# Second chunk's attention as a pinned pair-by-pair pipeline, keys' maxima by GpSimd, second weight converted by halves

## The chip, the cores and the metric

One core of a Trainium2 chip runs the kernel. The metric is the device time of one execution in microseconds. Engines of the core: TensorE (PE in the rows, its weight loads PEld), VectorE (DVE), ScalarE (ACT), GpSimd (POOL), and SyncE (SP), which here only issues DMAs. Each engine takes its own queue of instructions strictly in order; engines wait for each other by semaphores.

## The reference, cut to what matters

```python
q_s = softmax(q, over the head dimension)            # 8 batches, 8 heads, 576 tokens, 64 wide
k_s = softmax(k, over the 576 tokens)
kv = einsum('bhsd,bhse->bhde', k_s, v)
x = einsum('bhsd,bhde->bhse', q_s, kv)               # as 4608 tokens x 512
h = x @ w_in;  x = maximum(0.01 * h, h) @ w_out      # 512 -> 2048 -> 512, weights in float64
h = maximum(maximum(x @ w1, x @ w2), x @ w3); out = h @ w_out2   # 512 -> 768 -> 512
```

## The kernel before

The 4608 tokens stand in nine chunks of 512 (`NC`), a chunk reaching over one or two batches (`_pieces`). Heads go by pairs, so four pairs (`hp`) fill the 128 partitions. Attention of a batch and pair is a generator `kv_unit` (keys: maximum over the tokens, exponential, product with the values, division), that of a chunk and pair is `q_unit` (maximum, exponential, sum, division, four transposes on TensorE, product with the keys' result, split into a high and a low part, `xhi` and `xlo`). Products in float32 quality are three products of such parts (`mm3`): high by high, high by low, low by high.

The first wide product (w_in, w_out) is cut into 16 blocks (`MA`). Each block's weights come as 64-bit words in a tile `raw` and are converted by `split_words` to a high and a low part in a tile `w`, of which half `s = 0` belongs to w_in and half `s = 1` to w_out (`parts`). The conversion is one ScalarE pass (L172, absolute value), seven VectorE passes over 1024 columns (L173 to L185, with L184 the whole value and L185 the low part) and a ScalarE pass for the high part (L177); a ScalarE copy of half the whole values (L188) and a DMA from ScalarE's queue (L189) then keep w_in's whole values in HBM. All conversions use the one buffer `ca`.

A step is one block of one chunk: `project` (12 products of 512 columns into a bank `ps`), ScalarE's Prelu `g`, its parts `ghi` and `glo`, and `a_out` (12 products into four banks `acc`). `TURNS` sets the steps' order: chunk 0 with block 0 (step 0), then chunk 1 with blocks 0 and 1 (steps 1 and 2), chunk 0 with blocks 1 to 3 (steps 3 to 5), and so on; `BEGUN` says at which step the conversion of a block is begun. Chunk 0's attention runs first, alone. The attention of chunk 1 (batch 1, units in `second`) starts while step 0 runs; its units advance side by side, stage by stage (`advance`). After them the second block's conversion (`conv_a(1, ...)`) is written, then the third's.

In batch 0 and batch 1 the keys' maxima come from TensorE transposes (L415) and VectorE reductions (L420 to L422); for batch 1 they go back to all partitions as a diagonal times ones (L426, L429) and are added on VectorE (L431). From batch 2 on, VectorE takes the maximum of the five key tiles (L444, L446), GpSimd reduces it over the partitions (`partition_all_reduce`, L447), and VectorE subtracts (L452). The queues' order comes from a scheduler that works on the written order and its own forecast; instructions that are handed to `pin` (`keep_in_program_order`) keep their written order.

## Time and profile before

| What | us |
|---|---|
| median of 3 runs (1401.33 to 1402.17) | 1401.95 |
| profiled execution, whole time | 1401.96 |
| its span in the trace | 1400.1 |
| TensorE busy in the span | 1379.7 (99%) |
| VectorE busy | 865.4 (62%) |
| ScalarE busy | 673.3 (48%) |
| GpSimd busy | 156.4 (11%) |

The whole time is 1.86 us more than the span, and equals the median of the runs to 0.01 us. Times below are from the span's start. A duration in a row of the timeline is that of all instructions in the row from the first one's start to the last one's end; consecutive instructions of one engine overlap by some 0.08 us where the second doesn't need the first.

### The profile page before, as it was taken

What the parts mean: (1) busy time and instruction counts of PE and PEld (TensorE: products, weight loads), DVE (VectorE), ACT (ScalarE), POOL (GpSimd) and SP (SyncE); (2) the same over time, 40 slices, a digit from 0 to 9 for tenths busy, and PEclk for the clock granted to TensorE, in tenths of its full rate; (3) what the DMA queues carried; (4) which work ended last, traced back from release to release, by engine and by line L of the source; (5) the groups of instructions that cost most, each with busy time, mean ns of one, the idle gap of its engine ahead of it and who ended that gap; (6) DMA issues with size and microseconds to landing.
All of it is one profiled execution on the core that took longest, in us unless ns stands there. A gap on an engine that the chain in (4) does not pass through costs nothing.

```text
span 1400.1 us, 18335 instructions
## 1 busy us (share of the span) xinstructions
PE 1379.7 (99%) x6624; PEld 1127.8 (81%) x6624; DVE 865.4 (62%) x1500; ACT 673.3 (48%) x1387; POOL 156.4 (11%) x261
## 2 busy tenths in 40 slices
PE   7999999999999999999999999999999999999998
PEld 5788877788888788888888888888888888888887
DVE  9888978864786885656657455676457255434311
ACT  7766867754676656645445344334224224322211
POOL 0000202200111130110223300110010000000000
PEclk9999999999999999999999999999999999999999
DMA  9388864635977866768788797665673573554601
GB/s 368 129 284 305 300 224 132 220 108 206 386 287 269 366 215 233 285 215 351 242 338 326 284 359 268 237 225 173 228 260 135 210 293 120 173 218 158 237 26 38
DMA packets 90826, 330.10 MB, mean 236 GB/s; under 512 B 10672, under 2 KB 27056, under 8 KB 67568
## 3 DMA queue, kind: packets, MB, share of 16 engines
q1 hardware_dynamic: 68512, 251.46, 48.8%
q0 software_dynamic: 19056, 66.98, 14.0%
q10 hardware_dynamic: 3168, 10.49, 1.9%
q8 instruction: 52, 0.85, 0.2%
q14 instruction: 38, 0.31, 0.1%
HBM read 253.66 MB, written 75.24 MB: 235 GB/s over the span
## 4 chain that ended last, share of the span: by engine, by line
PE 89%; DVE 5%; ACT 3%; issue 1%; DMA 1%; POOL 0%; ACTq 0%; SPq 0%; DVEq 0%; POOLq 0%
PE ps L867 40%; PE acc L639 34%; PE ps L639 13%; PE ps L461 1%; PE ps L591 1%; ACT qo L527 0%; DVE glo L660 0%; DMA stream<-room 0%; DVE qmx L534 0%; DVE qsm L549 0%; DVE nmx L420 0%; ACT ghi L659 0%; DVE spare L546 0%; DVE spare L557 0%; PE ps L571 0%
## 5 line engine op out<-in xcount | busy, mean ns | idle before, releaser
L867 PE MATMUL ps<-op,group 128*128 128x512 f32 x1512 | 352.2, 389 | 0.0
L867 PEld LDWEIGHTS ps<-op,group 128*128 128x128 f32 x1512 | 283.7, 188 | 59.1 <-ACT snap L1099 0.2
L639 PE MATMUL acc<-ghi,outw 128*128 128x512 f32 x768 | 248.0, 391 | 0.9 <-ACT ghi L659 0.6
L867 PE MATMUL ps<-opA,group 128*128 128x512 f32 x1008 | 247.4, 391 | 0.8 <-ACT opA L827 0.6
L867 PEld LDWEIGHTS ps<-opA,group 128*128 128x128 f32 x1008 | 187.9, 188 | 41.5 <-ACT snap L995 1.5
L639 PEld LDWEIGHTS acc<-ghi,outw 128*128 128x128 f32 x768 | 143.7, 188 | 32.2 <-ACT ghi L659 1.6
L639 PE MATMUL acc<-glo,outw 128*128 128x512 f32 x384 | 150.5, 392 | 0.6 <-DVE glo L660 0.2
L639 PE MATMUL acc<-wo,h 128*128 128x512 f32 x558 | 135.6, 389 | 0.0
L639 PE MATMUL ps<-xhi,w 128*128 128x512 f32 x384 | 125.8, 394 | 1.3 <-ACT g L917 0.7
L639 PE MATMUL acc<-ghi,w 128*128 128x512 f32 x384 | 127.0, 393 | 0.0
L1099 ACT ACTIVATE snap<-ps 128x512 f32<-128x512 f32 x108 | 61.9, 597 | 134.6 <-PE ps L867 134.4
L639 PEld LDWEIGHTS acc<-wo,h 128*128 128x128 f32 x558 | 104.7, 188 | 21.8
L660 DVE TENSOR_TENSOR glo<-g,ghi 128x512 fp32r<-128x512 f32 x102 | 69.7, 687 | 74.4 <-ACT ghi L659 74.0
L1114 DVE TENSOR_TENSOR snap<-snap,ps 128x512 f32<-128x512 f32 x72 | 49.2, 685 | 93.2 <-ACT snap L1099 69.9
L639 PEld LDWEIGHTS ps<-xhi,w 128*128 128x128 f32 x384 | 72.1, 188 | 17.5 <-ACT g L917 1.1
L639 PEld LDWEIGHTS acc<-glo,outw 128*128 128x128 f32 x384 | 72.1, 188 | 17.3 <-DVE glo L660 2.6
L659 ACT ACTIVATE ghi<-g 128x512 fp32r<-128x512 f32 x102 | 63.4, 630 | 45.9 <-DVE g L1299 27.3
L639 PEld LDWEIGHTS acc<-ghi,w 128*128 128x128 f32 x384 | 71.8, 188 | 15.3
L1110 DVE TENSOR_TENSOR best<-snap,ps 128x512 f32<-128x512 f32 x36 | 24.7, 687 | 87.7 <-PE ps L867 39.2
L639 PE MATMUL acc<-glo,w 128*128 128x512 f32 x192 | 75.5, 393 | 0.8 <-DVE glo L660 0.8
L639 PE MATMUL ps<-xlo,w 128*128 128x512 f32 x192 | 74.9, 391 | 0.1
L1123 ACT ACTIVATE h<-best 128x512 fp32r<-128x512 f32 x48 | 30.3, 630 | 87.6 <-DVE best L1116 87.2
(188 smaller groups left out, 1917.2 us busy)
## 6 DMA issues: line engine op xcount, KB each, us to landing
group<-stream SPq DMA_DIRECT2D x62, 1024.0 KB, 6.2
outw<-stream_out SPq DMA_DIRECT2D x48, 1024.0 KB, 8.5
group<-stream_in SPq DMA_DIRECT2D x42, 1024.0 KB, 7.7
stream<-room POOLq DMA_DIRECT2D x66, 256.0 KB, 5.8
raw<-in_wa_dram SPq DMA_DIRECT2D x16, 1024.0 KB, 7.7
x<-st SPq DMA_DIRECT2D x40, 256.0 KB, 3.4
room<-in_wb_dram POOLq DMA_DIRECT2D x18, 512.0 KB, 8.0
stream_out<-w SPq DMA_DIRECT2D x16, 512.0 KB, 4.3
```

The costliest lines, as they stand in the source:

```text
L461: nc.tensor.matmul(acc[z, : D + 1], lhsT=ke[:, r, z], rhs=vt[:, r, h], start=r == 0, stop=r == RK - 1)
L591: nc.tensor.matmul(both(xps, c0, c1), lhsT=a, rhs=halves(y, c0, c1), start=i == 0, stop=i == 2)
L639: nc.tensor.matmul(acc, lhsT=l, rhs=r, start=first and i == 0, stop=last and i == 2)
L659: nc.scalar.activation(hi[:, z], g[:, z], AF.Copy)
L660: nc.vector.tensor_tensor(lo[:, z], g[:, z], hi[:, z].bitcast(F32), op=ALU.subtract)
L867: nc.tensor.matmul(bank, lhsT=l, rhs=r, start=fresh and first, stop=last, skip_group_check=not fresh)
L1099: nc.scalar.activation(t, bank, AF.Copy)
L1110: nc.vector.tensor_tensor(g, snap, bank, op=ALU.add)
L1114: nc.vector.tensor_tensor(snap, snap, bank, op=ALU.add)
L1123: nc.scalar.activation(h[:, m, 0], g, AF.Copy)
```

## The change

Five things are edited. First, `split_words` writes the whole values into the raw words' own tile, and their store goes out from SyncE's queue; ScalarE's copy is gone. Second, keys of batch 1 take the way of the later batches: four maxima per pair on VectorE, a reduction by GpSimd, one subtraction; the transposes, the diagonal and its product are gone for that batch. A reduction of one column is issued on GpSimd at the start. Third, the queries of chunk 1 are objects `EarlyQuery`, whose stages `finish_second` writes out in a fixed, pinned order, pair after pair, each pair's last stages among the next pair's first ones. Their loads are issued behind the loads of batch 1's keys and values and behind the store of block 0's whole values. Fourth, block 1 is converted by `split_by_halves`: the same operations, over 512 columns each, w_in's half before w_out's, with the high part made by VectorE (a cast) in place of ScalarE. Its VectorE work is written behind the last pair. Fifth, the four stores of step 0 are pinned, and so is the first product of step 2.

```diff
     def split_words(raw, hi, lo, n, after=None, whole=None, keep=None):
...
-        nc.vector.tensor_tensor(af, af, bf, op=ALU.add)
-        nc.vector.tensor_tensor(lo, af, hi.bitcast(F32), op=ALU.subtract)
+        z = raw.bitcast(F32)[:, :n]
+        nc.vector.tensor_tensor(z, af, bf, op=ALU.add)
+        nc.vector.tensor_tensor(lo, z, hi.bitcast(F32), op=ALU.subtract)
         if keep is not None:
-            copy = raw.bitcast(F32)[:, :N]
-            nc.scalar.activation(copy, af[:, :N], AF.Copy)
-            pin(nc.scalar.dma_start(keep, copy))
+            nc.sync.dma_start(keep, z[:, :N])
+    def split_by_halves(raw, hi, lo, keep):
...
+        for i in range(2):
+            z = slice(i * N, i * N + N)
+            pin(nc.scalar.activation(a[:, z].bitcast(F32), words[:, z, 1].bitcast(F32), AF.Abs))
+            yield
+        for i in range(2):
+            z = slice(i * N, i * N + N)
...
+            pin(nc.vector.tensor_scalar(af, af, MOST_HIGH, LEAST_HIGH, op0=ALU.min, op1=ALU.max))
+            nc.vector.tensor_scalar(au, au, 3, 0x3FFFFFF8, op0=ALU.logical_shift_left, op1=ALU.bitwise_and)
+            nc.vector.scalar_tensor_tensor(au, high, 0xC0000000, au, op0=ALU.bitwise_and, op1=ALU.bitwise_or)
+            nc.vector.tensor_copy(hi[:, z], af)
+            nc.vector.tensor_scalar(high, au, 0xFF800000, None, op0=ALU.bitwise_and)
+            nc.vector.scalar_tensor_tensor(bf, low, 2.0**-52, bf, op0=ALU.mult, op1=ALU.mult)
+            whole = raw.bitcast(F32)[:, 2 * i * N : 2 * i * N + N]
+            nc.vector.tensor_tensor(whole, af, bf, op=ALU.add)
+            nc.vector.tensor_tensor(lo[:, z], whole, hi[:, z].bitcast(F32), op=ALU.subtract)
+            if i == 0:
+                nc.sync.dma_start(keep, whole)
+        yield
...
+    pin(nc.gpsimd.partition_all_reduce(ones, ones, P, bass_isa.ReduceOp.max))
...
-        if b < FIRST:
+        if b == 0:
...
-            if b == 1:
-                diag = ap.tile([P, P], F32, tag="mx", name="diag", bufs=2)
-                nc.scalar.activation(diag, ident, AF.Copy, scale=mx[:, 0:1])
-                yield
-                spread = psum()
-                nc.tensor.matmul(spread[:, :P], lhsT=ones, rhs=diag, start=True, stop=True)
-                yield
-                nc.vector.tensor_tensor(ke, ke, spread[:, None, :P].to_broadcast([P, RK, P]), op=ALU.add)
-                nc.scalar.activation(ke, ke, AF.Exp)
...
+    class EarlyQuery:
...
+            nc.sync.dma_start(self.qt, q[1, hp])
+        def shift(self):
+            pin(nc.vector.tensor_reduce(mx, self.groups, axis=AX.X, op=ALU.max))
+            pin(nc.vector.tensor_tensor(self.groups, self.groups, self.spread(mx), op=ALU.subtract))
+            nc.scalar.activation(self.qt, self.qt, AF.Exp)
+        def normalise(self):
+            pin(nc.vector.tensor_reduce(sm, self.groups, axis=AX.X, op=ALU.add))
+            pin(nc.vector.tensor_scalar(sm, sm, EPS, None, op0=ALU.add))
+            pin(nc.vector.reciprocal(sm, sm))
+            pin(nc.vector.tensor_tensor(self.groups, self.groups, self.spread(sm), op=ALU.mult))
+            self.tp = psum()
+            for r in range(4):
+                pin(nc.tensor.transpose(self.tp[:, z], self.qt[:, z], ident))
+        def back(self):
+            pin(nc.scalar.activation(self.qt, self.tp, AF.Copy))
+        def multiply(self):
...
+        def high(self):
+            pin(nc.scalar.activation(xhi, self.xps, AF.Copy))
+            pin(nc.tensor.matmul(p, lhsT=minus, rhs=hi, start=False, stop=True, skip_group_check=True))
+        def low(self):
+                nc.vector.tensor_tensor(lo, p, hi.bitcast(F32), op=ALU.subtract)
+            pin(nc.scalar.activation(both(xlo, at, H), both(self.xps, at, H), AF.Copy))
...
+    def finish_second(keys, queries, convert):
+        keys = advance(keys, 2)
+        for z in queries[:2]:
+            z.shift()
+        advance(keys)
+        a_out(*prev, hold=True)
+        z = queries
+        z[0].normalise()
+        z[0].back()
+        z[2].shift()
+        z[0].multiply()
+        z[1].normalise()
+        z[0].high()
+        z[1].back()
+        z[0].low()
...
+        next(convert)
+        z[2].multiply()
+        z[3].normalise()
+        z[2].high()
+        z[3].back()
+        z[2].low()
+        z[3].multiply()
+        z[3].high()
+        z[3].low()
+        for _ in convert:
+            pass
...
-            acc = project(wA[m][0], x_tiles(c))
+            acc = project(wA[m][0], x_tiles(c), pinned=step == 2)
...
             if step == 0:
-                second = advance(second, 2)
-                a_out(*prev, hold=True)
+                finish_second(second_keys, second_queries, conv_by_halves(1))
                 prev = None
-                advance(second)
                 for f in range(KDM):
-                    store(f, x2[turn][:, f], accs[c][f], busy=True)
-                conv_a(1, spare(1, NP - 1))
+                    st = gp.tile([P, N], F32, tag="st", name="st", bufs=4)
+                    pin(nc.scalar.activation(st, accs[c][f], AF.Copy))
+                    nc.sync.dma_start(x2[turn][:, f], st)
                 conv_a(2, x_tiles(1)[0][:, NP - 1].bitcast(F32))
```

Three places of the built order show where instructions stand. Numbers are buffers: `w_416` (before) and `w_417` (after) hold block 0; `raw_445` with `w_724` (before) and `w_647` (after) hold block 1; `xhi_694`, `xlo_695` and `xhi_618`, `xlo_619` are chunk 1's parts; `ps_754`, `ps_787`, `ps_838` are the banks of steps 1, 2 and 3 before, and `ps_720`, `ps_752`, `ps_802` after; `spare_429` to `spare_438` (before) or `spare_435` (after) are the rooms of batch 1's four pairs.

VectorE, from the last division of batch 1's keys to the low part of block 1, before:

```order
L466 TENSOR_SCALAR rc_686<-ps_651 128x1
L467 RECIPROCAL rc_686<-rc_686 128x1
L173 TENSOR_SCALAR ca_725<-ca_725 128x1024
L174 TENSOR_SCALAR ca_725<-ca_725 128x1024
L175 SCALAR_TENSOR_TENSOR ca_725<-raw_445,ca_725 128x1024
L178 TENSOR_SCALAR raw_445<-ca_725 128x1024
L179 SCALAR_TENSOR_TENSOR raw_445<-raw_445 128x1024
L184 TENSOR_TENSOR ca_725<-ca_725,raw_445 128x1024
L623 TENSOR_TENSOR xlo_695<-ps_667,xhi_694 128x2x32
L623 TENSOR_TENSOR xlo_695<-ps_675,xhi_694 128x2x32
L623 TENSOR_TENSOR xlo_695<-ps_683,xhi_694 128x2x32
L185 TENSOR_TENSOR w_724<-ca_725,w_724 128x1024
```

The same place after, from the second pair's low part on:

```order
L669 TENSOR_TENSOR xlo_619<-ps_629,xhi_618 128x2x32
L632 TENSOR_REDUCE qsm_653<-spare_435 128x8
L633 TENSOR_SCALAR qsm_653<-qsm_653 128x8
L634 RECIPROCAL qsm_653<-qsm_653 128x8
L635 TENSOR_TENSOR spare_435<-spare_435,qsm_653 128x512
L669 TENSOR_TENSOR xlo_619<-ps_650,xhi_618 128x2x32
L669 TENSOR_TENSOR xlo_619<-ps_668,xhi_618 128x2x32
L202 TENSOR_SCALAR ca_648<-ca_648 128x512
L203 TENSOR_SCALAR ca_648<-ca_648 128x512
L204 SCALAR_TENSOR_TENSOR ca_648<-raw_445,ca_648 128x512
L205 CAST w_647<-ca_648 128x512
L206 TENSOR_SCALAR raw_445<-ca_648 128x512
```

Block 1's conversion, which stood ahead of all four low parts of chunk 1, now stands behind the last of them.

TensorE at the start of step 1, before:

```order
L619 MATMUL ps_667<-xhi_694,kvhi5_118 128x2x224
L619 MATMUL ps_675<-xhi_694,kvhi5_118 128x2x224
L619 MATMUL ps_683<-xhi_694,kvhi5_118 128x2x224
L619 MATMUL ps_691<-xhi_694,kvhi5_118 128x2x224
L639 MATMUL ps_754<-xhi_694,w_416 128x512
L639 MATMUL ps_754<-xlo_695,w_416 128x512
L639 MATMUL ps_754<-xhi_694,w_416 128x512 x2
L639 MATMUL ps_754<-xlo_695,w_416 128x512
L639 MATMUL ps_754<-xhi_694,w_416 128x512 x2
L639 MATMUL ps_787<-xhi_694,w_724 128x512
```

TensorE at the start of step 1, after:

```order
L648 MATMUL ps_668<-spare_435,plain_146 128x2x224
L715 MATMUL ps_720<-xhi_618,w_417 128x512
L715 MATMUL ps_720<-xlo_619,w_417 128x512
L715 MATMUL ps_720<-xhi_618,w_417 128x512 x2
L715 MATMUL ps_720<-xlo_619,w_417 128x512
L715 MATMUL ps_720<-xhi_618,w_417 128x512 x2
L715 MATMUL ps_720<-xlo_619,w_417 128x512
L715 MATMUL ps_720<-xhi_618,w_417 128x512
L662 MATMUL ps_668<-xhi_618,kvhi5_118 128x2x224
L715 MATMUL ps_720<-xhi_618,w_417 128x512
L715 MATMUL ps_720<-xlo_619,w_417 128x512
L715 MATMUL ps_720<-xhi_618,w_417 128x512
```

Nine of step 1's twelve products now stand ahead of the last pair's subtraction product (L662; L619 before), which its low part reads.

SyncE's queue of loads, before:

```order
L400 DMA spare_438<-in_k_dram 128x640
L513 DMA spare_438<-in_q_dram 128x512
L403 DMA spare_429<-in_v_dram 128x650
L403 DMA spare_432<-in_v_dram 128x650
L403 DMA spare_435<-in_v_dram 128x650
L403 DMA spare_438<-in_v_dram 128x650
L199 DMA raw_445<-in_wa_dram 128x1024
L199 DMA raw_447<-in_wa_dram 128x1024
```

And after:

```order
L428 DMA spare_435<-in_v_dram 128x650
L188 DMA wi0_149<-raw_185 128x512
L619 DMA spare_429<-in_q_dram 128x512
L619 DMA spare_431<-in_q_dram 128x512
L619 DMA spare_433<-in_q_dram 128x512
L619 DMA spare_435<-in_q_dram 128x512
L223 DMA raw_445<-in_wa_dram 128x1024
L223 DMA raw_447<-in_wa_dram 128x1024
```

The store of block 0's whole values, which waits for VectorE, now stands ahead of chunk 1's queries and of the raw words of blocks 1 and on.

## Rows read from the trace of the kernel before

**Rows 1.** Windows view: busy us (instructions) of each engine, clock, DMA share, GB/s.

```profile
60.00:70.00 10.00, 10.00 (x46) 7.99 (x45) 8.96 (x11) 6.51 (x12) 0.00 (x0) 1.00 0.49 180
```

**Rows 2.** Chain that ended last, from 46 us: start, us, engine, tile, line.

```profile
46.93 0.70 DVE ca L173
...
51.71 1.23 DVE ca L184
...
53.12 8.92 PE ps L639 x38
62.04 3.77 PE acc L639 x16
65.82 2.04 PE ps L639 x9
```

**Rows 3.** Timeline of VectorE: start, us, line, operation, tiles, shapes.

```profile
21.17 1.22 DVE L179 SCALAR_TENSOR_TENSOR raw<-raw 128x1024 f32<-128x1024 uint32 x1
...
62.66 1.22 DVE L185 TENSOR_TENSOR w<-ca,w 128x1024 fp32r<-128x1024 f32 x1
```

**Rows 4.** VectorE's groups by shape, first 200 us: busy us, mean ns of one.

```profile
L185 DVE TENSOR_TENSOR w<-ca,w 128x1024 fp32r<-128x1024 f32 x16 | 19.5, 1221 | 0.3
L660 DVE TENSOR_TENSOR glo<-g,ghi 128x512 fp32r<-128x512 f32 x26 | 17.9, 687 | 6.2 <-ACT ghi L659 5.9
L174 DVE TENSOR_SCALAR ca<-ca 128x1024 uint32<-128x1024 uint32 x16 | 11.1, 691 | 0.4
L446 DVE TENSOR_TENSOR mx<-mx,ke 128x128 f32<-128x128 f32 x12 | 3.4, 285 | 0.1
L452 DVE TENSOR_TENSOR ke<-ke,mx 128x640 f32<-128x640 f32 x4 | 3.2, 799 | 0.0
L556 DVE RECIPROCAL qsm<-qsm 128x8 f32<-128x8 f32 x12 | 2.3, 195 | 0.0
L467 DVE RECIPROCAL rc<-rc 128x1 f32<-128x1 f32 x12 | 1.9, 158 | 0.2
```

**Rows 5.** Timeline of TensorE, attention of chunks 0 and 1.

```profile
23.29 1.10 PE L571 MATMUL ps<-qf,plain 128*128 128x512 f32 x2 [0.42 <-issue]
...
39.62 0.60 PE L563 MATMUL ps<-ident,spare 128*128 128x128 f32 x4
...
52.08 0.48 PE L619 MATMUL ps<-xhi,kvhi 128*128 128x448 f32 x1 [0.67 <-ACT xhi L613]
...
67.47 0.39 PE L639 MATMUL ps<-xlo,w 128*128 128x512 f32 x1
```

**Rows 6.** Timeline of ScalarE, the same stretch.

```profile
37.77 1.58 ACT L669 ACTIVATE st<-acc 128x512 f32<-128x512 f32 x3
...
48.23 0.60 ACT L565 ACTIVATE qf<-ps 128x512 f32<-128x512 f32 x1
...
51.45 0.58 ACT L613 ACTIVATE xhi<-ps 128x512 fp32r<-128x512 f32 x1
```

**Rows 7.** DMA issues, first 40 us: KB each, median us to landing.

```profile
raw<-in_wa_dram SPq DMA_DIRECT2D x4, 1024.0 KB, 9.3
...
spare<-in_q_dram SPq DMA_DIRECT2D x8, 256.0 KB, 5.8
```

**Rows 8.** Timeline of all engines around two of GpSimd's reductions.

```profile
441.00 0.94 DVE L446 TENSOR_TENSOR mx<-mx,ke 128x128 f32<-128x128 f32 x3
...
442.12 0.70 POOL L447 PARTITION_ALL_REDUCE mx<-mx  x1 [5.87 <-ACT qo L527]
...
442.99 0.81 DVE L452 TENSOR_TENSOR ke<-ke,mx 128x640 f32<-128x640 f32 x1
...
499.14 1.22 DVE L828 TENSOR_TENSOR opA<-side,opA 128x1024 fp32r<-128x1024 f32 x1
499.41 2.12 POOL L447 PARTITION_ALL_REDUCE mx<-mx  x1 [8.21 <-DVE mx L446]
```

**Rows 9.** View of line L447: count, duration min/median/max in ns, first and last start.

```profile
L447 POOL PARTITION_ALL_REDUCE mx<-mx x24: 657/699/2121, 134.8 to 544.1; - x24
```

More of the change, by code (lines that the diff above doesn't have):

```diff
@@ L121, in tile_kernel @@
         nc.vector.tensor_tensor(ident[z, z], column[z, 0], column[z, 1], op=ALU.is_equal)
-    ones = const.tile([P, P], F32, name="ones")
+    ones = const.tile([P, 1], F32, name="ones")
     nc.gpsimd.memset(ones, 1.0)
@@ L406, in kv_unit @@
             yield
-        if b < FIRST:
-            t4, t1 = (ps_acc.tile([P, N], F32, tag="acc", name="t") if i == b == 0 else psum() for i in range(2))
+        if b == 0:
+            t4, t1 = (ps_acc.tile([P, N], F32, tag="acc", name="t") if i == 0 else psum() for i in range(2))
             back = ke.rearrange("p r d -> p (r d)")
@@ L450, in kv_unit @@
                 behind_step(vt[:, 0, 0, 0:1])
-            fetch.dma_start(vt, v[b, hp])
+            if b >= FIRST:
+                fetch.dma_start(vt, v[b, hp])
             nc.vector.tensor_tensor(ke, ke, mx[:, None, :].to_broadcast([P, RK, P]), op=ALU.subtract)
@@ L632, in split_kv, with mm3, project @@
         nc.vector.tensor_tensor(lo, full, hi.bitcast(F32), op=ALU.subtract)
-    def mm3(acc, a, b, first, last):
+    def mm3(acc, a, b, first, last, pinned=False):
         prods = ((a[0], b[0]), (a[0], b[1]), (a[1], b[0]))
         for i, (l, r) in enumerate(prods):
-            nc.tensor.matmul(acc, lhsT=l, rhs=r, start=first and i == 0, stop=last and i == 2)
+            ins = nc.tensor.matmul(acc, lhsT=l, rhs=r, start=first and i == 0, stop=last and i == 2)
+            if pinned and i == 0:
+                pin(ins)
     def cols(pair, i, n=P):
         return tuple(t[:, i * n : (i + 1) * n] for t in pair)
-    def project(wslot, xpair):
+    def project(wslot, xpair, pinned=False):
         acc = psum()
         for kk in range(KDM):
-            mm3(acc, cols(wslot, kk), tuple(t[:, kk] for t in xpair), kk == 0, kk == KDM - 1)
+            mm3(acc, cols(wslot, kk), tuple(t[:, kk] for t in xpair), kk == 0, kk == KDM - 1, pinned and kk == 0)
         return acc
@@ L730, in conv_a, with conv_by_halves @@
         wA[m] = parts(tiles[m])
+    def conv_by_halves(m):
+        raw = words.pop(m)
+        if raw.dtype != I64:
+            yield
+            yield
+            tiles[m] = weights(raw, None, whole_in[m])
+            yield
+        else:
+            w = tiles[m] = wp.tile([P, 2, 2, N], F32R, tag="w", name="w")
+            yield from split_by_halves(raw, flat(w[:, 0]), flat(w[:, 1]), whole_in[m])
+        wA[m] = parts(tiles[m])
     def plan_units(c):
@@ L793, in first_units @@
         return [unit(c, hp, True) for hp in range(NP) for unit in (kv_unit, q_unit)]
+    def finish_second(keys, queries, convert):
[13 more added lines that the diff above has]
+        z[0].low()
+        z[3].shift()
+        z[1].multiply()
+        z[2].normalise()
+        z[1].high()
+        z[2].back()
+        z[1].low()
+        next(convert)
[9 more added lines that the diff above has]
+            pass
     def advance(units, stages=99):
@@ L803, in tile_kernel @@
     conv_a(0, None)
-    second = advance(first_units(1), 2)
+    second_keys = [kv_unit(1, hp, True) for hp in range(NP)]
+    advance(second_keys, 1)
+    advance(second_keys, 1)
+    second_queries = [EarlyQuery(hp) for hp in range(NP)]
     load_a(1)
```

49 lines of the change are left out of this document (40 added, 9 removed).

## Prediction, made blind

> **What bounds the kernel now.** I read the windows first: from 60 us TensorE is busy for all of each window, at a granted clock of 1.00 [rows 1], its upper level of 2.4 GHz. A microsecond that it loses there isn't won back, and one that it gains in the stretch before is a gain of the whole. So the change acts by one thing: when TensorE begins its closed row of products, and whether the row stays closed. In the chain, step 1's first product starts at 53.12; before it stand VectorE's passes for block 1, from 46.93 to 52.94 [rows 2], and in VectorE's queue chunk 1's low parts stand behind them. Thus before, block 1's conversion delays `xlo`, and TensorE pays for it. But then block 1 is ready as the row begins, and block 2's low part at 63.88 [rows 3], before TensorE asks for it: behind 53.12 come 38, 16 and 9 products without a pause [rows 2], so the 63rd starts at 67.47 [rows 5], one every 0.227 us.
>
> The reader is to see two needs of TensorE that VectorE serves in a row: chunk 1's parts, and blocks 1 and 2. The change puts the parts first.
>
> **The point at which both are compared.** By the built order, 62 products of steps 1 to 4 stand ahead of the first that reads block 2's low part in the changed kernel. In the kernel before, the 63rd starts at 67.47. I work out when it can start after.
>
> **VectorE up to the queries.** Up to the end of L179, at 22.4 [rows 3], the queue is the same. Then: two passes over 1024 columns for block 0 at 1.22, less the overlap 0.08, 2.3 us; 16 maxima of 0.285 [rows 4], 0.20 apart where pairs alternate and 0.32 where one needs the one before, 4.2; four subtractions of 0.80 [rows 4], 3.0 with overlap; eight small divisions, 0.6. VectorE waits for GpSimd once, 0.3 (a reduction's result is used 1.05 us after its last maximum, 441.94 to 442.99 [rows 8], and the next pair's maxima cover most), and for the first product of keys with values, behind an exponential and TensorE's queue, 0.9. Sum 11.3: the queries begin at 33.7.
>
> **The queries.** Per pair: maximum, subtraction, sum and multiplication at 0.69 [rows 4], an addition of 0.16 and a reciprocal of 0.20, with overlaps and hand-offs of 0.04, 3.1 us. Four pairs 12.4, the low part `glo` of step 0 0.6, four divisions 0.3, two low parts `xlo` 0.3. Twice VectorE stands before `xlo`: the pinned order puts the next pair's four transposes (0.60) ahead of the subtraction product (0.48) [rows 5], which `xlo` needs, 1.0 each time. Sum 15.6: the fourth pair's multiplication ends at 49.3.
>
> **The last pair.** Now nothing overlaps: transposes 0.60, ScalarE's copy 0.60, products 1.1, the high part 0.58 [rows 5, 6], 0.2 of hand-offs. But the subtraction product, ready at 52.4, stands behind nine products of step 1, which start behind the last pair's product at 51.6 and take 9 x 0.227 = 2.0: 53.6. It takes 0.48, `xlo` 0.2 less the overlap: VectorE is free at 54.2. Step 1 begins earlier than before (51.6 against 53.12), but it isn't what decides.
>
> **Blocks 1 and 2.** Only now VectorE begins block 1, before at 46.93 [rows 2]. No row shows its half passes. A two-input pass over 512 columns takes 0.687; a one-input pass over 1024 takes 0.691 against 1.22 of the two-input one [rows 4], so 0.43 for 512 as my estimate. The cast lies between 0.43 and 0.69; I take 0.43, as it has one input. The first half: 0.43 + 0.43 + 0.69 + 0.43 and hand-offs, high part ready 2.1 after, at 56.3. TensorE asks for it behind step 1's last three products (about 55.3) and waits 1. Four products on, the second half of step 1 needs `g` and `ghi` (0.60 each), which stand on ScalarE behind four pinned copies of step 0, 0.5 apart [rows 6]: another wait of 1.3. These two waits don't add to the sum, since the one for block 2 comes later and ends last. The first half's eight passes take 4 x 0.43 + 4 x 0.69 = 4.5, hand-offs 0.2, less one overlap 0.1: low part ready after 4.6. The second half takes as long, two `glo` of 0.6 lie between: 54.2 + 4.6 + 4.6 + 1.2 = 64.6. Block 2 is seven passes, as block 1 before: 46.93 to 52.94 for six of them [rows 2] and 1.22 [rows 4], 7.2, so its low part is ready at 71.8.
>
> Hand-offs cost more than 0.04 where engines take turns: the same kind of sum for the kernel before, from 22.4 on, gives 51.9 where the row has 53.12 [rows 2]. The new chain has as many turns; I add the 1.2. The 63rd product then starts at 73.0 instead of 67.47: **5.5 us late**.
>
> **Whether that stays.** Later conversions are begun by steps of TensorE (they wait for `g`), so they move with it; the products behind are the same. Neither a gain nor another loss: 1401.96 + 5.5 = **1407.5 us**, and as the profiled execution equals the median to 0.01 us, the same against the median.
>
> **Edits at nothing.** The transposes and the diagonal's product that go lie where TensorE waits anyhow. ScalarE's copies that go free an engine that isn't waited for in the closed row. The stores that move to SyncE wait there for VectorE: the first until 23.9, and behind it the queries and blocks 1 to 3. The queries' loads are issued by 25.8 and land 5.8 later [rows 7], the first by 30.2, asked for at 33.7; the last by 31.6, asked for ten us later. Block 1, issued at 26.3, lands by 35.6 (9.3 [rows 7]) and is read by ScalarE near 48. If that cover of 3.5 us were gone, each us beyond it would be paid in full. GpSimd's reduction at the start runs where GpSimd has nothing else until the first maximum.
>
> **GpSimd beside VectorE.** One reduction took 0.70, another 2.12 with a 1.22 us two-input pass of VectorE beside it [rows 8]. The next sentences may be skipped. The Trainium skill, "SBUF — State Buffer", section "SBUF: two separate sides", says that GpSimd and VectorE share a pair of ports under an exclusive lock, which a VectorE operation with two SBUF inputs takes against a GpSimd operation that reads SBUF, and that the loser is held for the whole instruction. By that rule every reduction here would be held, since VectorE is full of such passes then; the 2.12 agrees, the 0.70, inside a stretch with such passes too, is not far enough from free to show it.
>
> **Rivals.** (1) The forecast, chance 0.66: 1405.8 to 1409.2, for hand-offs that cost 0 to 2.4 more than the sum where I took 1.2, and the cast's bounds of 0.26 for each half. (2) Part of it is hidden, 0.13: if a half pass takes half of a whole one (16 of them 7.8 instead of 9.2) and hand-offs cost no more than my sum, TensorE loses 5.5 - 1.4 - 1.2 = 2.9, 1404.9; without VectorE's two waits ahead of the queries (1.2) 1403.7. For it: whole passes run at that rate; against it: every small pass pays a fixed part, 0.158 for one column [rows 4]. (3) Not slower, 0.06: blocks 1 and 2 come in time, and step 1's earlier start stands, 51.6 + 1.2 = 52.8 against 53.12: 1401.6. The point from which it decides is the end of VectorE's last `xlo`: 54.2 - 5.5 = 48.7. Against it: VectorE's own work from 22.4 to the last pair's multiplication, without any wait, is 10.1 + 13.6 = 23.7 and ends at 46.1, and the last pair's chain of 4.9 comes behind it, 51.0. For it speaks only that no row shows the pinned order at work. A gain of over 2.8 us would need more still, 0.03 of the 0.06. (4) GpSimd is held, 0.15: each reduction takes 2.12 instead of 0.70 [rows 8]. Four serial ones add 5.7, of which maxima and divisions cover 1.7: 4.0 more, 1411.5. For it the 2.12; against it the median of 24, 699 ns [rows 9]. This is the rule of the page above, priced by the row. That the change doesn't do what it says is not a rival of its own: the built order has the pairs and the halves as written.
>
> **How the numbers follow.** Predicted is the likeliest, 1407.5. The range leaves out (3), the lower part of (2) and the end of (4): 1404.4 to 1411.2. About 0.2%, 2.8 us, is what a measurement of this kernel can tell from no change, so faster means under 1399.1 and slower over 1404.8. (1) and (4) are slower, 0.81, with a little of (2), 0.02; the rest of (2) and half of (3) are the same, 0.14; faster 0.03.
>
> **What would show it.** In the changed kernel's chain: VectorE's first pass over 512 columns (L202) starts near 55 instead of block 1's at 46.93; step 1's first product starts at or before 53; TensorE shows waits of about 1 us for the cast (L205) and for `g`, and near 70 one of 2 to 3 us for block 2's low part (L186); from there on its windows are full, at a constant distance to before. Wrong would be the forecast if L202 starts by 50, if TensorE's windows from 55 to 75 are full, or if the reductions are followed by waits of VectorE of over 1 us each (rival 4).

## The result: 1408.76 us, slower by half a per cent

The changed kernel takes 1408.76 us (median of 6 runs, 1407.85 to 1412.70) against 1401.70 us for the kernel before (6 runs, 1401.23 to 1402.17): ratio 1.0052, 95% interval 1.0039 to 1.0065. Its profiled execution is the fastest of its runs, 1407.85 us with a span of 1405.8. Before's was 1401.96, so between the two profiles lie 5.89 us.

Where they go is read first from the windows of the changed kernel (stretch, its length, then busy us and instructions of TensorE, its weight loads, VectorE, ScalarE, GpSimd; granted clock, DMA share, GB/s):

```profile
40.00:50.00 10.00, 5.77 (x26) 3.14 (x26) 7.58 (x19) 5.57 (x10) 0.00 (x0) 1.00 0.05 17
50.00:60.00 10.00, 6.75 (x27) 4.14 (x26) 5.02 (x11) 6.41 (x12) 0.00 (x0) 1.00 0.18 67
60.00:70.00 10.00, 9.96 (x44) 8.23 (x45) 9.39 (x16) 3.64 (x6) 0.00 (x0) 1.00 0.54 187
70.00:80.00 10.00, 7.33 (x33) 5.77 (x32) 9.56 (x11) 6.50 (x12) 0.00 (x0) 1.00 0.80 298
80.00:90.00 10.00, 10.00 (x46) 8.29 (x45) 8.73 (x10) 4.79 (x8) 0.00 (x0) 1.00 0.69 244
```

TensorE stands still for 4.2 us of the first ten, 3.3 of the next, and 2.7 between 70 and 80; from 80 on it is full, as it was from 60 on before [rows 1]. VectorE too stands still for half of 50 to 60, and is full behind that. The chain that ended last shows the hand-overs (start, us, engine, tile, line). Its first line is the nine products of step 1, 2.07 us, that stand ahead of the last pair's subtraction product:

```profile
53.21 2.07 PE ps L715 x9
55.27 0.22 PE ps L662
...
55.51 0.24 DVE xlo L669
...
56.88 1.95 ACT st L1056 x4
...
58.84 0.49 ACT g L1044
...
66.13 0.69 DVE ca L173
...
72.15 1.24 DVE w L186
...
73.43 2.56 PE ps L715 x10
```

Block 2's first pass, L173, begins at 66.13, where before block 1's began at 46.93 and block 2's low part was ready at 63.88 [rows 2, 3]. TensorE's timeline (in brackets: idle before the instruction, and what ended it) gives its four waits behind the pairs; the last line is also the 63rd product, at which the prediction compares, and which was at 67.47 before [rows 5]:

```profile
56.37 0.50 PE L715 MATMUL ps<-xlo,w 128*128 128x512 f32 x1 [0.67 <-ACT xlo L670]
...
57.87 0.47 PE L715 MATMUL ps<-xhi,w 128*128 128x512 f32 x1 [0.76 <-DVE w L205]
...
60.04 1.19 PE L715 MATMUL acc<-ghi,w 128*128 128x512 f32 x4 [1.01 <-ACT ghi L737]
...
73.43 0.73 PE L715 MATMUL ps<-xhi,w 128*128 128x512 f32 x2 [2.67 <-DVE w L186]
```

73.43 - 67.47 = 5.96 us, and the whole execution is 5.89 longer: what is lost by then stays lost in the sum. That the two agree so closely is a balance. Behind the 63rd product the changed kernel loses 0.9 more at one place, where a product waits for `glo`:

```profile
154.04 0.51 PE L715 MATMUL acc<-glo,w 128*128 128x512 f32 x1 [0.72 <-DVE glo L738]
```

and the kernel before has a pause of 0.7 near 250 and a smaller one near 528 that the changed kernel doesn't have (TensorE busy 57.54 of the 60 us from 200 on before, 58.30 after). VectorE's own timeline at three places of the new order:

```profile
34.73 0.68 DVE L626 TENSOR_REDUCE qmx<-spare 128x8 f32<-128x512 f32 x1
...
55.51 0.23 DVE L669 TENSOR_TENSOR xlo<-ps,xhi 128x64 fp32r<-128x64 f32 x1 [3.83 <-PE ps L662]
55.66 0.42 DVE L202 TENSOR_SCALAR ca<-ca 128x512 f32<-128x512 f32 x1
...
57.30 0.43 DVE L205 CAST w<-ca 128x512 fp32r<-128x512 f32 x1
```

The line with 3.83 is the heart of it: VectorE, the engine that is late, waits 3.83 us for the last pair's subtraction product, with sixteen passes over block 1 and seven over block 2 queued behind that wait.

### The profile page after: what moved, and what is told of

It reads as the page before. It is cut to its first block, busy times and chain, and to the rows that moved or that the text cites. A ratio compares the mean times of both kernels' runs of the same rounds, so it can differ in the third digit from the quotient of the medians.

```text
span 1405.8 us, 18273 instructions
## 1 busy us (share of the span) xinstructions
PE 1376.7 (98%) x6596; PEld 1123.3 (80%) x6596; DVE 867.0 (62%) x1513; ACT 662.7 (47%) x1366; POOL 162.4 (12%) x266
## 3 DMA queue, kind: packets, MB, share of 16 engines
q1 hardware_dynamic: 70816, 255.66, 50.2%
## 4 chain that ended last, share of the span: by engine, by line
PE 89%; DVE 5%; ACT 3%; DMA 2%; issue 1%; SPq 0%; ACTq 0%; DVEq 0%
PE ps L994 40%; PE acc L715 33%; PE ps L715 11%; PE ps L607 1%; PE ps L477 1%; DMA raw<-in_wa_dram 1%; DVE glo L738 1%; PE ps L587 0%; ACT ghi L737 0%; DMA ke<-in_k_dram 0%; ACT qo L543 0%; DMA spare<-in_q_dram 0%; DVE ca L175 0%; DVE qmx L550 0%; ACT ca L172 0%
## 5 line engine op out<-in xcount | busy, mean ns | idle before, releaser
L715 PEld LDWEIGHTS ps<-xhi,w 128*128 128x128 f32 x384 | 72.0, 188 | 20.9 <-DVE w L186 3.1
```

The lines of the kernel that those rows point to most:

```text
L715: ins = nc.tensor.matmul(acc, lhsT=l, rhs=r, start=first and i == 0, stop=last and i == 2)
```

## The experiments

Two theories stood at the start. **Queue:** the loss is the length of VectorE's queue behind the last `xlo`; whatever takes passes out of it, or puts them into VectorE's idle pieces, gives back as much. **Pipeline:** the pinned pairs cost the time by themselves (queries 11 us later), or GpSimd or SyncE does. After the first four runs a third came up, **clock**.

**1. The first half ahead of the last `xlo`.** Each half's passes follow its absolute values, and the first half is called between two pairs:

```diff
             pin(nc.scalar.activation(a[:, z].bitcast(F32), words[:, z, 1].bitcast(F32), AF.Abs))
             yield
-        for i in range(2):
-            z = slice(i * N, i * N + N)
             au, high, low = a[:, z], words[:, z, 1], words[:, z, 0]
...
         z[2].low()
+        next(convert)
         z[3].multiply()
```

> The changed kernel with one edit: VectorE's eight passes over block 1's first half stand ahead of the last xlo subtraction (between the third pair's low part and the fourth pair's product) and no longer behind it. Theory, queue length: the 63rd product comes late because both halves of block 1 and all of block 2 stand behind the last xlo on VectorE, which the rows show idle for 3.83 us ahead of that subtraction. The first half takes 4.58 us (57.30 less 1.64 to 59.55 + 0.69): 3.8 of it goes into the hole, 0.8 pushes the last xlo. Block 2 ends 3 to 4 us earlier, the 63rd product at 69.5 to 70.5 in place of 73.43, the execution at 1404 to 1405 in place of 1407.85. Rival, the pipeline: what costs is that the queries are begun 11 us later in place of beside the keys; then an order behind the queries changes nothing, and the time stays at 1407.5 to 1408. Rival, GpSimd or SyncE: no change either.

Measured: 1405.22 us in one execution (before in the same job 1402.15), just above the 1404 to 1405 expected, with half clock from 49.4 to 52.8. It was then timed:

> The changed kernel with the first half ahead of the last xlo, now timed. Theory, queue length: 2.5 to 3.5 us below the changed kernel in the same job; with the clock falling between 49 and 53 us as in the one look it loses some 1.5 of that again in some executions. Rival, that the profile of the one look was a lucky execution: level with the changed kernel within 1 us.

Measured: 1406.65 us (6 runs, 1404.36 to 1408.46), ratio 1.0036 (1.0024 to 1.0048), where the changed kernel in the same job took 1411.53: 4.9 us less, more than the 2.5 to 3.5 expected of the queue. The profiled execution of these, VectorE and TensorE:

```profile
56.08 0.69 DVE L208 TENSOR_TENSOR w<-raw,w 128x512 fp32r<-128x512 f32 x1
56.69 0.22 DVE L667 TENSOR_TENSOR xlo<-ps,xhi 128x64 fp32r<-128x64 f32 x1
...
70.70 0.73 PE L713 MATMUL ps<-xhi,w 128*128 128x512 f32 x2 [1.08 <-DVE w L186]
```

The first half's last pass (L208) now stands ahead of the last `xlo`, which comes 1.2 us later than in the changed kernel; the 63rd product comes at 70.70 instead of 73.43, 2.7 us earlier. The execution is at 1404.36 instead of 1407.85, 3.5 us earlier, and 0.9 of that is the changed kernel's wait at 154 us, which this profile doesn't have. So an order on VectorE alone, with the pipeline as it is, moves TensorE by 2.7 us: the queue holds, and the pipeline alone doesn't explain the loss. The rest of the 4.9 us between the medians no trace shows.

**2. Block 1's arithmetic left out.**

```diff
-            pin(nc.vector.tensor_scalar(af, af, MOST_HIGH, LEAST_HIGH, op0=ALU.min, op1=ALU.max))
...
-            nc.vector.tensor_tensor(lo[:, z], whole, hi[:, z].bitcast(F32), op=ALU.subtract)
+            pin(nc.vector.tensor_copy(hi[:, z], af))
+            nc.vector.tensor_copy(lo[:, z], hi[:, z].bitcast(F32))
```

> The changed kernel without block 1's conversion on VectorE: of sixteen passes over its halves four copies stand, which write hi and lo without the words' own arithmetic (the values of this block are not the reference's, and the part that is stored for later is hi). Theory, queue length: with some 7.5 us less behind the last xlo, block 2 ends near 64, no product of step 1 waits for a weight, and what is left is the attention's own lateness (last xlo 55.51 here, step 1's end 58.3) against before: 63rd product at 68.3 to 69, execution at 1402.5 to 1404, which is 0.5 to 2 us above before. Rival, that the pinned pipeline costs most of the 5.9 us by itself: 1406 or more.

Measured: 1406.73 us, outside what the queue theory gave and inside its rival's. TensorE's timeline shows that the queue's part was right all the same, since nothing waits for block 1 any more and for block 2 only 0.38 us, and the windows show what was not in either theory:

```profile
71.03 0.73 PE L708 MATMUL ps<-xhi,w 128*128 128x512 f32 x2 [0.38 <-DVE w L186]
```
```profile
40.00:50.00 10.00, 5.95 (x25) 3.18 (x23) 7.06 (x16) 5.10 (x11) 0.00 (x0) 0.88 0.10 32
50.00:60.00 10.00, 9.13 (x30) 6.09 (x31) 3.68 (x10) 5.44 (x11) 0.00 (x0) 0.78 0.09 31
```

The granted clock is 0.88 and 0.78 there, 1.00 in the changed kernel's profile. From 47.6 to 54.4 us TensorE ran at its lower level of 1.2 GHz, and the third and fourth pair came later by it: the last `xlo` at 57.71 instead of 55.51 (0.6 of these 2.2 us stood there before the first pair's `xlo`). And one product waits where the changed kernel's doesn't:

```profile
532.39 2.32 PE L987 MATMUL ps<-opA,group 128*128 128x512 f32 x9 [1.07 <-ACT snap L1114]
```

Without the 2.2 us and the 1.2 that this place costs, the time would be 1403.3, inside what the queue theory gave; that is worked out from one execution. As an answer to queue against pipeline this run is spoiled by the clock and by that wait.

**3. Halves undone.**

```diff
-                finish_second(second_keys, second_queries, conv_by_halves(1))
+                finish_second(second_keys, second_queries, iter([None]))
...
+                conv_a(1, spare(1, NP - 1))
                 conv_a(2, x_tiles(1)[0][:, NP - 1].bitcast(F32))
```

> The changed kernel with the halves undone: block 1 is converted in one piece behind the pipeline, as before. Theory, queue length: one piece of seven VectorE passes and ScalarE's copy is some 1.5 us shorter on VectorE than two halves with eight passes each, but no product can use it until it is whole, TensorE has nothing from 56.8 on and block 2 starts behind ScalarE's first pass over it: the 63rd product at 74 to 75 and 1408.5 to 1409.5, so the halves gave back about 1 us. Rival, that the halves are the cost (two more VectorE passes in all, eight fixed costs more): 1406 to 1407.

Measured: 1412.31 us. I had the place wrong: without the pins of the halves, block 1's passes don't stand behind the pairs but among them. VectorE's timeline, then TensorE's:

```profile
38.95 0.69 DVE L173 TENSOR_SCALAR ca<-ca 128x1024 f32<-128x1024 f32 x1 [0.27 <-ACT ca L172]
...
47.65 1.23 DVE L186 TENSOR_TENSOR w<-raw,w 128x1024 fp32r<-128x1024 f32 x1
```
```profile
43.63 0.63 PE L639 MATMUL ps<-ident,spare 128*128 128x128 f32 x4 [3.11 <-DVE spare L635]
...
49.86 1.09 PE L639 MATMUL ps<-ident,spare 128*128 128x128 f32 x4 [2.63 <-DVE spare L635]
...
51.68 2.29 PE L648 MATMUL ps<-spare,plain 128*128 128x64 f32 x4 [0.36 <-ACT spare L642]
```

Block 1's passes, from 38.95 to 48.88, hold up the first and second pair's transposes by 3.11 and 2.63 us. Into these holes fell the clock: four transposes take 0.63, and 1.09 six us later; the windows of 40 to 70 have 0.71, 0.50 and 0.76. So the run says nothing on what the halves are worth; it shows that whoever goes first on VectorE, block 1 or the pairs, the other pays.

**4. The order mended.** Block 1's half passes go, one or two at a time, into all four of VectorE's idle pieces, ScalarE's four copies between its own pieces of the pairs, and the last subtraction product ahead of step 1's second group:

```diff
         z[1].normalise()
+        next(convert)
         z[0].high()
         z[1].back()
+        next(convert)
+        next(convert)
         z[0].low()
+        next(copies)
...
         z[3].multiply()
+        next(convert)
+        next(convert)
         z[3].high()
+        next(copies)
+        next(convert)
         z[3].low()
```

> The changed kernel with its order mended: block 1's sixteen half passes are laid one to two at a time into VectorE's four idle pieces (1.02, 1.02, 0.95 and 3.83 us ahead of the four xlo subtractions), ScalarE's four copies of step 0's sums go into its idle pieces too, and the last pair's subtraction product stands ahead of step 1's second group of products. Nothing else differs. Theory, queue length: of 9.2 us of conversion some 6 us find idle time, block 2 ends near 65.5 and no product waits for it; 63rd product 0.3 to 1 us behind before's, execution at 1402 to 1403.2. Rival, the pipeline itself costs: 1405 or more.

Measured: 1405.69 us; its windows have a granted clock of 0.92 and 0.57 from 40 to 60, with half clock from 48.3 to 58.6. At that level 10 us do the work of 5 at most. The same order timed again (under 5) ran in 1402.29 to 1402.41 us in its three executions with a mean clock of 0.999, where this one had 0.995: so some 3 us of the time are the clock's, and without them it would stand near where it was expected. That is worked out, and the next runs ask it.

**5. The clock asked directly.** The changed kernel gets 20 products that nobody reads, put where TensorE waits between its pairs:

```diff
             self.tp = psum()
+            self.fill(self.tp, (0, 3, 7, 2)[self.hp])
             for r in range(4):
...
+        def fill(self, t, n):
+            for _ in range(n):
+                pin(nc.tensor.matmul(t, lhsT=wA[0][0][0][:, :P], rhs=x_tiles(0)[0][:, 0], start=True, stop=True))
...
         def back(self):
+            self.xps = psum()
+            self.fill(self.xps, 2)
             pin(nc.scalar.activation(self.qt, self.tp, AF.Copy))
```

> The changed kernel with 20 further TensorE products of 128x512 between its pairs' transposes and products (3, 7 and 2 ahead of three groups of transposes, 2 ahead of each pair's product; their results are overwritten and nothing reads them), laid where TensorE waits anyway: 20 times 0.227 us = 4.5 us of work in some 5.5 us of waiting, so by durations the kernel is 0 to 0.4 us longer. What it asks: after's executions run from 1407.85 to 1412.7 at a mean granted clock of 0.999 to 0.993, and in four runs of this study the granted clock fell to 0.50 at 44 to 49 us, after TensorE had been busy 5 to 7 of 10 us, and stayed there 3 to 20 us. Theory, clock: it is the holes in that stretch that let the clock fall, in some executions earlier and longer than in others; with the holes filled the fall is gone, the executions agree within 0.5 us, and their median is 1407.8 to 1408.4, below after's 1408.76. Rival, that the scatter has nothing to do with these holes: executions from 1408 to 1413 as in after, and half clock near 45 to 60 us again.

> The mended order (block 1's half passes and step 0's copies in the idle pieces, the last subtraction product early) together with the 20 further TensorE products. Theory, queue length and clock together: the mended order alone was at half clock from 48.7 to 58.3 us and lost some 4 us to it; with the clock held it ends at 1402 to 1403, 0.3 to 1 us above before, in all executions alike. Rival, that the pinned pipeline costs more than its holes and its clock: 1404 to 1406. Rival, that the fall doesn't come from the holes: 1405 to 1407, scattered.

> The changed kernel as it is, beside the two next ones on one chip. Theory, queue length and clock: its mechanism is worth 5.5 to 6 us, and on top the clock falls in the stretch of holes in some executions and not in others; its executions lie 5.5 to 11 us above before's median, their lower end near before + 5.7, the mean clock 0.993 to 0.999 and lower where the time is longer. Rival, that the time is the queue alone: executions within 1.5 us of each other, at before + 6.

> The mended order without the further products, again, now timed. Theory, clock: the one look fell to half clock from 48.3 to 58.6 us; other executions do so for shorter or longer, so they scatter over 3 to 5 us with the clock, from about 1402 to 1406, while the same order with the further products lay within 1402.8 to 1404.6. Rival, the order alone: within 1.5 us.

The first two ran in one job (before 1402.27, 21 runs, 1401.57 to 1403.72), the last two in another (before 1401.81, 22 runs, 1401.09 to 1402.85):

| Kernel | Median us | From to | Ratio (interval) | Mean clock |
|---|---|---|---|---|
| changed, again | 1411.53 | 1408.85 to 1413.05 | 1.0068 (1.0055 to 1.0080) | 0.994 to 0.997 |
| changed, 20 products more | 1411.23 | 1410.53 to 1411.69 | 1.0063 (1.0050 to 1.0076) | 0.996 to 0.998 |
| mended order, again | 1403.46 | 1402.29 to 1406.88 | 1.0013 (1.0004 to 1.0022) | 0.994 to 0.999 |
| mended order, 20 products more | 1404.18 | 1402.79 to 1404.59 | 1.0011 (1.0002 to 1.0020) | 0.996 to 0.999 |

The mended order takes some 8 us off the changed kernel (1411.53 to 1403.46 in one job), more than the queue's 5.9, and its scatter of 4.6 us goes with the clock, as expected: 1402.29 to 1402.41 at a mean clock of 0.999, 1402.96 to 1404.06 at 0.998 and 0.997, 1405.03 at 0.995, 1406.88 at 0.994. What is left, 1.65 us above before, stays with the pinned pipeline; no run pulls it apart. For the clock, compare the window of 70 to 80 of the changed kernel's profile above, 7.33 us busy with 33 products at 1.00, with that of its second profile:

```profile
50.00:60.00 10.00, 8.41 (x29) 5.01 (x28) 4.29 (x11) 5.83 (x12) 0.00 (x0) 0.83 0.04 16
...
70.00:80.00 10.00, 7.35 (x22) 5.58 (x21) 9.51 (x11) 7.02 (x11) 0.00 (x0) 0.70 0.92 339
```

As busy, but with 22 products: the clock fell at 74.1, during the wait for block 2, and the row of products began at half speed. That execution took 1411.12 us with the same order of instructions. It had its 63rd product at 74.77 (1.3 us later, with half clock from 36.5 to 40.0 and from 50.2 to 53.6), and the fourteen products from there on took 6.1 us instead of 3.3. Of these 4.2 us 3.3 are left in the whole execution: the first profile loses 0.9 at 154 us, which the second doesn't (TensorE busy 69.27 of 70 us from 130 to 200 there, 70.00 in the second). So the same kernel costs 5.9 us by its queue in one profile and, by the clock, 4.2 more in the other. The other nine executions have no trace: they run up to 1413.05, 5 us above the first profile, at lower mean clocks than its 0.999, but at one mean clock of 0.995 from 1409.26 to 1413.05. That their time is the clock's is likely and not shown.

The further products did in their stretch what was expected, and in sum they did not. Their windows, first of the changed kernel with them, then of the mended order with them:

```profile
40.00:50.00 10.00, 9.32 (x44) 5.98 (x43) 7.69 (x17) 5.60 (x12) 0.00 (x0) 1.00 0.11 37
...
70.00:80.00 10.00, 7.34 (x26) 5.55 (x25) 9.52 (x11) 7.39 (x12) 0.00 (x0) 0.83 0.88 329
```
```profile
40.00:50.00 10.00, 9.32 (x43) 5.97 (x42) 9.34 (x21) 7.11 (x15) 0.00 (x0) 1.00 0.17 61
50.00:60.00 10.00, 9.31 (x42) 6.85 (x41) 8.91 (x18) 6.37 (x13) 0.00 (x0) 1.00 0.47 170
```

With TensorE busy 9.3 of 10 us from 40 to 50 (then 8.3 and 9.3) the clock stays at 1.00 from 40 to 60 in both, where six of the eight profiles of orders with the holes show a fall between 44.2 and 50.2; and the executions agree within 1.2 and 1.8 us instead of 4.2 and 4.6. But the changed kernel's next hole, the wait for block 2, is still there, and behind it the clock falls (0.83 in 70 to 80). My expected 1407.8 to 1408.4 was missed by 3 us, and the theory that the holes between the pairs are the whole of it fell. The profiled execution, 1411.69, is 3.84 above the changed kernel's first profile: its 63rd product is 0.9 later (0.8 of that was there before the pairs began), half clock from 75.5 to 78.9 takes 1.7, and one wait of 1.4 near 538 us for a ScalarE copy, which the first profile doesn't have, makes it 4.0. That wait is there in two more profiles (1.07 in experiment 2, 0.79 in the mended order with the products) and has nothing to do with the clock. What the other four executions lost, no trace shows; it is hardly the clock alone, since two of them took 1410.53 and 1411.36 at a mean clock of 0.998, the changed kernel 1407.95 at 0.997. In the mended order the products gained nothing in the median either; it is 1.2 us above what I expected and inside the rival's range for a pipeline that costs by itself. The wait of 0.79 near 529 is about 1 us of that in the profiled execution, and in the profile step 1's row of products still has a pause in it (the last subtraction product waits 0.69 for `xhi`).

**6. The kernel before with two parts of the change.** Summed words with SyncE's store, and GpSimd's maxima for the second chunk's keys; no pipeline, no halves:

```diff
-        nc.vector.tensor_tensor(af, af, bf, op=ALU.add)
-        nc.vector.tensor_tensor(lo, af, hi.bitcast(F32), op=ALU.subtract)
+        z = raw.bitcast(F32)[:, :n]
+        nc.vector.tensor_tensor(z, af, bf, op=ALU.add)
+        nc.vector.tensor_tensor(lo, z, hi.bitcast(F32), op=ALU.subtract)
...
-        if b < FIRST:
+        if b == 0:
```

> The kernel before with two parts of the change and not the others: whole values are summed into the raw words and stored by SyncE (ScalarE's copy and its store go), and the second chunk's keys' maxima are made by GpSimd. The pipeline by pairs, the pinned order and the halves are left out. Theory, queue length: these two parts cost nothing, they take ScalarE's copies (0.6 us each) and the transposes and reductions of the keys out of the first 50 us; step 1 begins 0.5 to 0.8 us earlier and the execution is at 1401 to 1401.7, so the whole loss belongs to the pipeline with its order. Rival, GpSimd or SyncE: 1403 to 1406.

> Before with the summed words, SyncE's store and GpSimd's maxima alone, now timed. Theory: these two parts are worth 0.3 to 0.8 us (its one look came out level with before, but with its first conversion 1.3 us later than in before's profile); ratio 0.9993 to 0.9998. Rival, they are worth nothing or cost: ratio 1.0000 to 1.0015.

Measured: 1402.32 us in one execution; timed, 1401.84 (11 runs, 1400.98 to 1403.19), ratio 1.0000 (0.9992 to 1.0009). The two parts cost nothing, so the whole loss belongs to the pipeline with its order and the halves; the gain of 0.3 to 0.8 that I expected isn't there.

**7. And two instructions moved.** In before, ScalarE's copy of block 1's high parts (1.06 us, at 50.48) stands ahead of the last `xhi` at 51.45 [rows 6], and two VectorE passes over block 1 (L179, and L184 [rows 2]) ahead of the first `xlo` subtraction. From before's timelines:

```profile
50.38 1.23 DVE L179 SCALAR_TENSOR_TENSOR raw<-raw 128x1024 f32<-128x1024 uint32 x1
...
50.48 1.06 ACT L177 ACTIVATE w<-ca 128x1024 fp32r<-128x1024 f32 x1
```

The copy and L179 are each tied behind one instruction of the attention (the tie orders an engine's queue and adds no wait):

```diff
         if whole is None:
-            nc.scalar.activation(hi, af, AF.Copy)
+            behind(nc.scalar.activation(hi, af, AF.Copy), "xhi")
...
-        nc.vector.scalar_tensor_tensor(bf, low, 2.0**-52, bf, op0=ALU.mult, op1=ALU.mult)
+        behind(nc.vector.scalar_tensor_tensor(bf, low, 2.0**-52, bf, op0=ALU.mult, op1=ALU.mult), "xlo")
...
+            ins = nc.scalar.activation(lo, p, AF.Copy)
+            if (c, hp) == (1, NP - 1):
+                marks["xhi"] = ins
...
+                if (c, hp) == (1, 0):
+                    marks["xlo"] = ins
```

> As the run without the pipeline, and two instructions of block 1's conversion set behind the second chunk's attention: ScalarE's copy of block 1's high parts (1.05 us) behind the last xlo copy, and VectorE's product of the low words (1.23 us) behind the first xlo subtraction. In before both stand ahead and hold step 1's first products. Theory, order of the queues: step 1 begins about 1.2 us earlier than without that edit, nothing later waits for block 1, and the execution is at 1400 to 1400.8: 1.2 to 1.8 us below before, with a clock as in before since TensorE stays busy 8 to 9 of 10 us. Rival, that block 1's lateness takes it back: 1401.2 to 1402.

Measured: 1400.16 us (11 runs, 1399.36 to 1401.64) against 1402.27 in the same job, ratio 0.9986 (0.9977 to 0.9995). It is faster than both kernels, by 2 us against before. TensorE's timeline, this kernel and then the one of experiment 6:

```profile
51.99 0.50 PE L643 MATMUL ps<-xhi,w 128*128 128x512 f32 x1 [0.23 <-DVE xlo L625]
```
```profile
52.84 0.50 PE L632 MATMUL ps<-xhi,w 128*128 128x512 f32 x1 [0.23 <-DVE xlo L616]
```

Step 1 begins 0.85 us earlier, with no wait for block 1 or 2 behind it, and the start is no reason for it: VectorE's last pass over block 0 begins at 25.73 here and at 25.68 there. Against before's 53.12 [rows 2] it is 1.1 earlier. So some 0.9 us are shown to come from the order. The rest of the 2.1 us in the median is open: between this profile and the timed one of experiment 6, 0.9 us more lie behind TensorE's last product, which starts 4.2 us before the end here and 5.1 there (4.0 to 4.7 in before, the changed kernel and experiment 6's first profile). The goal of the change (the attention ahead of block 1) is thus reached, as far as it pays here, with two moved instructions instead of all of block 1.

## Why the prediction was right, step by step

Predicted was 1407.5 us (1404.4 to 1411.2); measured 1408.76, and 1407.85 in the profiled execution. Its steps against the changed kernel's profile:

| Step | Predicted | Trace |
|---|---|---|
| queries begin on VectorE | 33.7 | 34.73 |
| fourth pair's multiplication ends | 49.3 | 50.51 |
| VectorE free behind the last `xlo` (L202 begins) | 54.2 | 55.66 |
| block 1's second half ready | 64.6 | 66.13 |
| block 2's low part ready | 71.8 | 73.38 |
| 63rd product (with 1.2 for hand-offs) | 73.0 | 73.43 |
| late against before | 5.5 | 5.96 |

**The stretch to the queries** is where the sum was short, by 1.0 us. L179 ended 0.3 later, at 22.73; the waits took 0.20 for GpSimd and 1.07 and 0.41 for the products of keys with values, 1.7 where I had 1.2; and one subtraction took 1.03 us instead of 0.81. **The queries** took 15.8 of the predicted 15.6, **the last pair** 5.2 of 4.9, **block 1** 10.5 of 10.4, **block 2** 7.3 of 7.2. Without the 1.2 us that I added at the end for turns between engines the sum would have been 1.6 short. They were of about the right size: waits took 0.5 more than the sum ahead of the queries, and the four parts behind ran over by 0.1 to 0.3 each, 0.55 together. The 0.4 that is left is the later end of L179 and the slow subtraction, which they weren't meant for.

**The unseen sizes.** The cast of 512 columns took 0.43 us, the lower of its bounds and the one I took; the one-input half pass 0.42, estimated at 0.43. The waits of 0.76 for the cast and 1.01 for `ghi` came as predicted (1 and 1.3) and, as predicted, don't add to the end: L186's wait of 2.67 came last. Step 1's first product was at 52.70, before 53.12, and that decided nothing.

**The rivals.** GpSimd was not held. Its reductions for the four pairs:

```profile
26.61 1.40 POOL L462 PARTITION_ALL_REDUCE mx<-mx  x2 [22.53 <-DVE mx L461]
...
30.63 1.41 POOL L462 PARTITION_ALL_REDUCE mx<-mx  x2 [2.62 <-DVE mx L461]
```

0.70 each, like most of [rows 9] and unlike the 2.12 of [rows 8]. But the effect is real, and the prediction had its premise wrong: VectorE was not full of long two-input passes there. Beside these reductions it ran maxima of 0.28 us. Where a long two-input pass was under way as a reduction began, it was held, in this same execution:

```profile
158.37 0.68 DVE L738 TENSOR_TENSOR glo<-g,ghi 128x512 fp32r<-128x512 f32 x1
158.50 2.25 POOL L462 PARTITION_ALL_REDUCE mx<-mx  x1 [4.25 <-DVE qsm L569]
158.97 1.22 DVE L186 TENSOR_TENSOR w<-raw,w 128x1024 fp32r<-128x1024 f32 x1
```

The reduction ends at 160.75, 0.56 behind the end of the second pass. The Trainium skill, "SBUF — State Buffer", section "SBUF: two separate sides", would have it held for the length of such a pass. The trace agrees here; for the four pairs it shows no hold. It works the other way as well: VectorE's first subtraction, beside the second reduction, is the one that took 1.03, 0.2 more than the others. Partly hidden and not slower fell with the sizes above: the point at which "not slower" would have decided, a last `xlo` done by 48.7, was missed by 7 us.

**What it didn't have.** "Neither a gain nor another loss" behind the 63rd product holds for the first profile only in the sum (0.9 lost at 154 us, about as much not lost that before loses), which is luck, and not for the kernel. The prediction read the clock of a full window of before and said nothing of the clock in the holes that it forecast. The median of the first six runs lies 0.9 above the profiled execution, and that of the second job is 1411.53, just outside the range. So it was right by mechanism and by the size of the queue, and short by a term for the clock: 4.2 us in the one profile that shows it, nothing in the other, perhaps up to 5 in executions without a trace.

## What to carry to other kernels

When a change reorders a busy engine's queue, add up what then stands behind the reordered piece and find the first consumer of each result; a wait inside the queue (here 3.83 us) is paid by everything behind it. Moving the one or two instructions that really hold the critical chain can reach the aim, where moving the whole block turns one lateness into another. And where a forecast opens holes in TensorE's row, give it a second term: what the next products cost at half clock, with the scatter between executions that this brings.

## What the runs showed of the hardware

**The granted clock fell in the stretch with holes, in some executions and not in others.** Same program, two profiles: 1.00 throughout from 40 to 90 us in one; in the other 0.50 from 36.5 to 40.0, from 50.2 to 53.6 and from 74.1 to 80.9. No single pause of TensorE ahead of the fall at 50.2 was longer than 1.8 us; it was busy 6.2 of the 10 us from 40 to 50. In the profile without a fall it was busy 5.8 of the same ten, so that alone doesn't tell the two apart. Held busy 9.3 of 10 there, two kernels showed no fall in that stretch, in one profile each. The Trainium skill, "TensorE: Matmul & The Clock Gate", section "HAM oscillation — how this bites in real kernels", describes the same thing for waits on DMA: the next burst of products starts at the lower clock. The second profile agrees (22 products instead of 33 in a window as busy), the first, with a wait of 2.67 us at the same place, doesn't; the page's waits were DMA's, these are VectorE's. What it is that makes one execution fall and another not, no run here shows.

**GpSimd's reductions and VectorE's long passes held each other.** Where a two-input pass of VectorE over 512 or 1024 columns was under way as a reduction began, the reduction mostly ended 0.56 us behind it: it took 2.25 and 1.64 us in the changed kernel (at 158.50 and 170.01), 2.12 in before [rows 8] and 1.07 in the kernel of experiment 6 (at 33.17), against 0.66 to 0.71 where nothing held it. At 279.35 in the changed kernel it was the other way: the reduction took 0.66, and the pass under way (L263) 1.61 in place of 1.22. An estimate of what a GpSimd instruction takes needs the pass that stands beside it.

**The start scatters.** VectorE's last pass over block 0 began at 24.64 in the changed kernel's first profile and at 25.43 in that with the further products, though the programs are alike up to there; half clock from 14.0 to 20.9 instead of 14.1 to 17.5 goes with it. Differences below 1 us between single executions of this kernel mean nothing unless they are counted from a common event.
